# Local attention's operands loaded from channel rows in quarters of 32 partitions, and a high part written in place

## The chip, the cores and the metric

The kernel runs on one core of a Trainium2 chip. The core has a matrix engine (TensorE, PE in the profile; its loads of stationary operands are PEld), three engines for vectors (VectorE, DVE; ScalarE, ACT; GpSimd, POOL) and SyncE (SP), which here issues nearly all DMA transfers. Each engine carries out its own instructions in order; semaphores hold them together. Sixteen DMA engines move the data. The metric is the time of one execution on the device, in microseconds (us); the median of three runs is the kernel's time.

## What is computed

Two attentions with separate inputs and weights, set side by side in the output. Both have 32 heads of 18 channels over 2048 positions; all is float32.

```python
def _A_ref(x, wqkv, wo):                 # x [1, 2048, 576]
    H = 32; Dh = D // H
    W, dil = 8, 2
    qkv = (x @ wqkv).reshape(B, S, 3, H, Dh).transpose(2, 0, 3, 1, 4)
    q, k, v = qkv[0], qkv[1], qkv[2]
    idx = pos[:, None] - off[None, :]    # off = 0, 2, 4 .. 14
    logits = jnp.einsum("bhsd,bhswd->bhsw", q, kg) * scale
    logits = jnp.where(mask[None, None, :, :], logits, -1e9)
    attn = _softmax(logits, axis=-1)
    o = jnp.einsum("bhsw,bhswd->bhsd", attn, vg)
    return o.transpose(0, 2, 1, 3).reshape(B, S, D) @ wo

def _B_ref(x, wqkv, wo):
    ...
    scores = jnp.einsum("bhqd,bhkd->bhqk", q, k) * scale
    p = _softmax(scores, axis=-1)
    o = jnp.einsum("bhqk,bhkd->bhqd", p, v)
    return o.transpose(0, 2, 1, 3).reshape(B, S, D) @ wo

return jnp.concatenate([a, b], axis=-1)
```

A is a local attention: each position looks at itself and at seven earlier positions, two apart (14 positions back at most; kg and vg are keys and values gathered so). B is a full attention.

## The kernel before

**Precision.** Matrix products run in a reduced float32 format. Operands are split into a high part (rounded by a copy) and a low part (the rest), and products are summed as high by high, high by low and low by high.

**Projections (to about 422 us).** x comes in transposed, 576 channels by 2048 positions, in five pieces of rows per 512 positions: four of 128 channels and a last one of 64. For each such group of positions the function `inputs` (L393) loads the pieces and splits them: `split` (L371) rounds on ACT (L372) and subtracts on VectorE or POOL (L373). The last 64 channels are loaded twice, into both halves of the partitions; one half of the tile `xhl` keeps the high part (L407), the other half the low part: ACT writes the high part into a tile `ohi` (L408), and the difference goes to `xhl` (L409). `ohi` has four buffers, which this step shares with the results of the projections: `leave` (L459) copies B's queries and keys out of PSUM (L464), rounds them into `ohi` (L465), takes the low part on POOL (L466) and stores both (L471); `leave_a` (L652) copies a part of A's projection into `ohi` (L654) and stores it to `da` in DRAM (L655). A buffer is free again when its store has landed. The tile `more` holds the raw rows of the last 512 positions of A. `da` has one row per channel: 576 of queries, 576 of keys, 576 of values, each 14 zeros and then 2048 positions.

**Scores (from about 424 us).** B runs in 512 steps: 8 groups of four heads, 4 blocks of 512 queries each, 16 tiles of 128 keys. In a step PE makes four score tiles (L232), which ACT turns into exponentials (L238), and weighs values with those of an earlier step (L704, into `po`). With them PE makes three or four tiles of scores for a later block (L162), of which VectorE takes the maxima (L169); the maxima are turned, split on POOL (L107, L108) and placed beside the queries by eight small loads (L195). Every 16 steps a block ends: ACT copies `po` to `o` (L713), SP loads the four rows of denominators into `den` (L736), due one step later; eight steps after the block's end VectorE takes their reciprocals (L737), SP stores them (L738) and loads them back spread over the partitions as `rec` (L739, due at 13), and POOL multiplies (L740, 18), splits (L741, L742), and SP stores (L732, 26). Twelve loads bring each later group's queries and keys (`stack_loads`, L146 and L147), and one its values (L247).

**A beside B.** A has eight blocks of 256 positions, 54 steps apart, from step 10 + 54 j. Partitions are 32 heads times 4 quarters of 64 positions: partition 32 s + h holds quarter s of head h. For each block the function `local` (L818) plans pieces by step:

- `arrange` (L823): three DMA copies, DRAM to DRAM, from `da` into `dparts`, one each for queries, keys and values. A copy has 576 channels times 4 quarters, each a run of 64 positions (queries) or 78 (keys and values, with the 14 positions before). They are due 24 steps ahead of the block or, where that falls into the first 14 steps of a group, later.
- `fetch` (L829): one load of 128 long rows per tensor (L833), into `aq` (one buffer) and `akv` (two buffers, keys and values by turns); queries at step 0 of the block, keys at 1, values at 28.
- `match`, from step 5: products of queries and keys on POOL (L844) and their sums (L848), last the logits `lg` (L851). VectorE takes maxima over the window (`am`, L862, from step 31), POOL subtracts (L868), ACT takes exponentials, VectorE sums and inverts (L878), POOL scales (L881).
- `weighted`, from step 39: products with the values (L887) and sums (L888 to L890) on POOL; then the split and the stores to `dao` (L902), from which `get` (L912, L914) loads `at` and `ahl` for the product with A's output weights (L1014).

**What sets the order.** Nearly the whole program is written out by hand: `plan` and `later` put functions under step numbers, and `due` calls them in that step. All loads above stand in SP's one queue in that order. A DMA waits on SP for what it needs and, as eight semaphores are used by turns, for the DMA eight places ahead of it; everything behind it waits too.

Of the kernel before, what the change touches and what calls it, by code (L numbers as in the profile page):

```python
# [7 lines left out]
F32 = mybir.dt.float32  # L8
F32R = mybir.dt.float32r
BF16 = mybir.dt.bfloat16  # L10
AF = mybir.ActivationFunctionType
# [5 lines left out]
S = 2048  # L17
D = 576
H = 32
DH = 18  # L20
# [9 lines left out]
NJ = S // AB  # L30
SUB = AB // 4
HALO = DIL * (W - 1)

STEPS = NB * NT
# [9 lines left out]
GAP = 54  # L44

A_FROM = 10
# [5 lines left out]
def ap(t, *dims):  # L52

    return bass.AP(tensor=t.tensor, offset=t.offset, ap=[list(t.ap[0])] + [list(d) for d in dims])


def rows(t, *dims):

    return bass.AP(tensor=t.tensor, offset=t.offset, ap=[list(d) for d in dims])
# [3 lines left out]
def two_attentions(ctx: ExitStack, tc, xa, wa, woa, xb, wb, wob, out):  # L63
# [5 lines left out]
    nc = tc.nc  # L69
    load = nc.sync.dma_start  # L70

    const = ctx.enter_context(tc.tile_pool(name="const", bufs=1))
    dram = ctx.enter_context(tc.tile_pool(name="dram", bufs=1, space=DRAM))
# [9 lines left out]
    def bank(kind=None):  # L83
# [6 lines left out]
    dqk = dram.tile([2, 2 * D, S], F32, name="dqk")  # L90
    dv = dram.tile([NG, 128, NT, 4 * 19], F32, name="dv")


    da = dram.tile([3 * D, HALO + S], F32, name="da")
    dparts = [[dram.tile([4, D, (HALO if n else 0) + SUB], F32, name=f"dpart{n}{j}") for n in range(3)]
              for j in range(NJ)]
    dao = dram.tile([NJ, 2, 4, D, SUB], F32, name="dao")
    drec = dram.tile([NG, NB, 4, 512], F32, name="drec")
    do = dram.tile([2, NG - 1, 128, S], F32, name="do")
# [242 lines left out]
    with (tc.tile_pool(name="x", bufs=1, side="right") as xp,  # L342
# [14 lines left out]
        def staged(src, cols, dims, into, spare=False):  # L357

            n = sum(m for _, m in cols)
            wide = src.shape[1]  # L360
            raws = {}

            def get(c, issue=load):
                t = raws[c] = raw(spare)
                for at, r0, m in [(0, 128 * c, 128)] if c < 4 else [(0, 512, 64), (64, 512, 64)]:
                    issue(ap(t[at : at + m], (n // len(cols), len(cols)), (1, n // len(cols))),
                          rows(src[r0, cols[0][0]], (wide, m), *dims))

            return get, lambda c: into(c, raws[c][:, :n])

        def split(engine, hi, lo, t):  # L371
            nc.scalar.activation(hi, t, AF.Copy)  # L372
            engine.tensor_sub(lo, t, hi)  # L373
# [19 lines left out]
        def inputs(src, b, engine, spare=False):  # L393
            x = [[], [], None]

            def into(c, t):
                if c < 4:
                    hi, lo = (xp.tile([128, 512], F32R, name=nm, bufs=4 * NB) for nm in ("xhi", "xlo"))
                    x[0].append(hi)
                    x[1].append(lo)  # L400
                    split(engine, hi, lo, t)
                else:

                    hl = x[2] = xp.tile([128, 512], F32R, name="xhl", bufs=NB)
                    high = xp.tile([128, 512], F32R, name="ohi", bufs=4)
                    one, other = (slice(64 * (b % 2), 64 * (b % 2) + 64), slice(64 - 64 * (b % 2), 128 - 64 * (b % 2)))
                    nc.scalar.activation(hl[one], t[one], AF.Copy)  # L407
                    nc.scalar.activation(high[other], t[other], AF.Copy)  # L408
                    engine.tensor_sub(hl[other], t[other], high[other])  # L409

            return x, *staged(src, [(512 * b, 512)], [(512, 1), (1, 512)], into, spare)

# [30 lines left out]
        qkv, odd = ExitStack(), ExitStack()  # L443
# [3 lines left out]
        if True:  # L447
# [34 lines left out]
            for c in range(5):  # L482
                one, other = (load, nc.scalar.dma_start) if c % 2 == 0 else (nc.scalar.dma_start, load)
# [159 lines left out]
            for k in range(2, 14):  # L643
                n = 46 if k == 2 else 36 + 4 * k
# [7 lines left out]
            def leave_a(c, b, n, ps):  # L652
                o = xp.tile([128, 512], F32, name="ohi", bufs=4)
                nc.scalar.activation(o[:n], ps, AF.Copy)  # L654
                load(da[128 * c : 128 * c + n, HALO + 512 * b : HALO + 512 * b + 512], o[:n])  # L655
# [23 lines left out]
            for c, b in order:  # L679
                n = min(128, 3 * D - 128 * c)  # L680
                work_list.append(((b % 2, ws[c][0], xas[b][0], slice(0, n), every),
                                  lambda ps, n=n: ps[:n], lambda ps, c=c, b=b, n=n: leave_a(c, b, n, ps)))
# [16 lines left out]
    work = ctx.enter_context(tc.tile_pool(name="work", bufs=1, reuse_waits="tile"))  # L699
# [118 lines left out]
    def local(j):  # L818

        st = {}  # L820
        p0 = AB * j

        def arrange(n):  # L823
            wide = (HALO if n else 0) + SUB
            load(rows(dparts[j][n][0, 0], (wide, D), (D * wide, 4), (1, wide)),
                 rows(da[D * n, HALO + p0 + SUB - wide :], (HALO + S, D), (SUB, 4), (1, wide)))


        def fetch(nm):  # L829
            halo = 0 if nm == "q" else HALO  # L830
            n = DH * (halo + SUB)
            t = st[nm] = work.tile([128, DH, halo + SUB], F32, name="akv" if halo else "aq", bufs=2 if halo else 1)
            load(ap(t, (1, n)), rows(dparts[j]["qkv".index(nm)][0, 0], (n, 128), (1, n)))  # L833

        def window(t, c):

# [46 lines left out]
        def weighted(c):  # L883
            if c == 0:
                st["o"] = work.tile([128, DH, SUB], F32, name="ao", bufs=1)
            at = wide()
            nc.gpsimd.tensor_mul(at, ap(st["lg"], (0, 2), (SUB, W), (1, SUB)), window(st["v"], c))  # L887
            nc.gpsimd.tensor_add(at[:, :, :4], at[:, :, :4], at[:, :, 4:])  # L888
            nc.gpsimd.tensor_add(at[:, :, :2], at[:, :, :2], at[:, :, 2:4])  # L889
            nc.gpsimd.tensor_add(st["o"][:, 2 * c : 2 * c + 2], at[:, :, 0], at[:, :, 1])  # L890
# [10 lines left out]
        def put(i):  # L901
            load(rows(dao[j, i, 0, 0], (DH * SUB, 128), (1, DH * SUB)),  # L902
                 ap(st["parts"][i].bitcast(F32), (1, DH * SUB)))
# [18 lines left out]
        def sums_of_a(h):  # L922
# [3 lines left out]
            if h == 0:  # L926
# [3 lines left out]
            nc.scalar.activation(y, two, AF.Copy)  # L930
            behind_scores.append(lambda: nc.vector.tensor_add(y, one, y))

        pieces = [(0, lambda: fetch("q")), (1, lambda: fetch("k")), (28, lambda: fetch("v")), (33, lower),
                  (35, exponents), (39, share), (60, upper), (61, rest), (64, lambda: put(0)), (66, lambda: put(1))]

        pieces[:0] = [(at, lambda f=f, n=n: f(n)) for f, ats in ((most, (31, 32, 33)), (total, (36, 37, 38)),
                                                                (inverses, (38, 39))) for n, at in enumerate(ats)]
        for c in range(DH // 2):
            pieces.append((5 + 5 * c // 2, lambda c=c: match(c)))
            pieces.append((39 + 5 * c // 2, lambda c=c: weighted(c)))  # L940
        at = A_FROM + GAP * j - 24

        at = max(at, STEPS * (at // STEPS) + 14) - A_FROM - GAP * j
        for n in range(3):
            pieces.append((at + n if j else n - 7, lambda n=n: arrange(n)))
        made = [p - A_FROM - GAP * j for p in MADE[j]]
        for n, ends in enumerate((made[:2], made[2:])):
            pieces.append((max(ends[0] - 8, made[1] + 1 if n else 0), lambda n=n: get(n)))
# [145 lines left out]
    for j in range(NJ):  # L1094
        plan(A_FROM + GAP * j, local(j))
# [15 lines left out]
    rest = NG * NB * PIECES * 2 - early  # L1111
# [24 lines left out]
    while step < ALL:  # L1136
        n, kt = divmod(step, NT)
# [51 lines left out]
```

## Time and profile before

| what | value |
|---|---|
| runs | 1648.64, 1649.69, 1653.81 us |
| median | 1649.69 us |
| profiled execution: its time | 1651.53 us |
| profiled execution: span, first to last instruction | 1649.8 us |
| mean granted TensorE clock | 0.995 |
| bytes read from and written to HBM | 113.16 and 88.12 MB |
| DMA packets, of these under 512 B | 188353, 118384 |

Rows of the profile are read so. A group or a timeline row has the line of the code, the engine, the operation, what is written from what, and how often ("x"). In a timeline the first number is the start in us from the span's start and the second the length; brackets at the end tell how long the engine stood idle before and what released it. SPq rows are DMA issues: their length is the time that SP needed for the issue, not that of the transfer. Rows of tiles give the shortest, median and longest duration in ns and the first and last start. Rows of stretches give the start and end, the length, then the busy time of PE, PEld, DVE, ACT and POOL, each with its number of instructions, then the granted clock (1.00 is full), the DMA engines' busy share and GB/s. "bank" is a PSUM bank with a score or product tile.

### The profile page before, as it was taken

The numbers are of one execution on the slowest core, as the hardware profiler recorded it, in microseconds if no ns is written. First come the engines' busy times: TensorE is split into PE (matmuls) and PEld (weight loads), VectorE is DVE, ScalarE is ACT, GpSimd is POOL, SyncE is SP. The second block draws the span as 40 slices with busy tenths as digits, with TensorE's granted clock in tenths as the row PEclk, the third lists the DMA queues.
The fourth block names the chain that finished last, engine by engine and source line by source line (L and its number), as shares of the span: only waits on it lengthen the run. The fifth ranks groups of instructions, "written<-read, shape, count | busy, mean of one in ns | idle before, by whom it ended". The sixth has DMA issues, their size and how long they took to land.

```text
span 1649.8 us, 33746 instructions
## 1 busy us (share of the span) xinstructions
PE 1632.9 (99%) x12906; PEld 951.6 (58%) x12906; DVE 1392.9 (84%) x2366; ACT 1224.0 (74%) x2419; POOL 960.1 (58%) x792
## 2 busy tenths in 40 slices
PE   9999999999999999999999899999999999999998
PEld 7999879999433444444444344444444444445676
DVE  5199989999899888889888789899899989888533
ACT  7314432111899999999999799999999999998554
POOL 2306642210195996995994993995995997930000
PEclk9999999999999999999999899999999999999999
DMA  9937954522515347167228325826626141033201
GB/s 257 232 113 208 251 164 134 137 89 90 95 47 101 97 120 128 54 150 124 74 66 158 96 82 119 150 74 97 151 87 109 65 133 51 21 121 117 106 37 59
DMA packets 188353, 188.22 MB, mean 114 GB/s; under 512 B 118384, under 2 KB 132208, under 8 KB 186464
## 3 DMA queue, kind: packets, MB, share of 16 engines
q1 hardware_dynamic: 183328, 174.53, 41.6%
q0 software_dynamic: 4032, 10.63, 3.3%
q8 instruction: 101, 1.65, 0.5%
q10 hardware_dynamic: 832, 0.92, 0.2%
q14 instruction: 60, 0.49, 0.1%
HBM read 113.16 MB, written 88.12 MB: 122 GB/s over the span
## 4 chain that ended last, share of the span: by engine, by line
PE 90%; POOL 6%; DMA 1%; DVE 1%; issue 1%; ACT 0%; SPq 0%; POOLq 0%; ACTq 0%; DVEq 0%
PE po L704 27%; PE bank L232 22%; PE bank L325 16%; PE bank L162 13%; PE bank L1014 7%; PE bank L262 5%; POOL pr L844 1%; POOL pr L887 1%; POOL pr L848 1%; DMA den<-o 1%; DVE mx L169 1%; POOL pr L888 1%; POOL pr L889 0%; DMA dqk<-ohi 0%; PE bank L478 0%
## 5 line engine op out<-in xcount | busy, mean ns | idle before, releaser
L169 DVE TENSOR_REDUCE mx<-bank 128x1 f32<-128x512 f32 x2048 | 1287.8, 684 | 146.0 <-PE bank L162 115.4
L238 ACT ACTIVATE e<-bank 128x512 f32<-128x512 f32 x2048 | 1062.1, 606 | 97.0 <-PE bank L232 57.3
L162 PE MATMUL bank<-ks,qs 54*128 54x512 f32 x2048 | 753.5, 423 | 7.1 <-DVE mx L169 6.9
L232 PEld LDWEIGHTS bank<-qs,ks 56*128 56x128 f32 x2048 | 328.4, 186 | 447.4 <-ACT e L238 417.7
L232 PE MATMUL bank<-qs,ks 56*128 56x512 f32 x2048 | 573.0, 426 | 0.0
L704 PE MATMUL po<-e,v 128*19 128x512 f32 x4096 | 538.4, 600 | 0.0
L162 PEld LDWEIGHTS bank<-ks,qs 54*128 54x128 f32 x2048 | 341.3, 185 | 18.0 <-DVE mx L169 11.4
L704 PEld LDWEIGHTS po<-e,v 128*19 128x19 f32 x4096 | 70.6, 97 | 185.7 <-issue 182.9
L844 POOL TENSOR_TENSOR pr<-aq,akv 128x1024 f32<-128x1024 f32 x72 | 158.5, 2202 | 28.1 <-PE bank L232 25.5
L887 POOL TENSOR_TENSOR pr<-lg,akv 128x1024 f32<-128x1024 f32 x72 | 158.3, 2198 | 0.6
L848 POOL TENSOR_TENSOR pr<-pr 128x1024 f32<-128x1024 f32 x64 | 152.5, 2383 | 5.0
L654 ACT ACTIVATE ohi<-bank 128x512 f32<-128x512 f32 (+1 forms) x56 | 30.5, 595 | 147.2 <-issue 115.9
L325 PE MATMUL bank<-xhi,ahi 64*128 64x512 f32 (+1 forms) x448 | 114.3, 390 | 3.1 <-ACT ohi L654 3.1
L325 PE MATMUL bank<-xhi,alo 64*128 64x512 f32 (+1 forms) x448 | 113.3, 390 | 0.0
L325 PE MATMUL bank<-xlo,ahi 64*128 64x512 f32 (+1 forms) x448 | 111.2, 390 | 0.2 <-POOL xlo L373 0.2
L888 POOL TENSOR_TENSOR pr<-pr 128x512 f32<-128x512 f32 x72 | 92.4, 1283 | 5.6
L373 POOL TENSOR_TENSOR alo<-raw,ahi 128x512 fp32r<-128x512 f32 (+1 forms) x14 | 17.6, 1255 | 121.5 <-ACT ahi L372 88.9
L466 POOL TENSOR_TENSOR olo<-olo,ohi 128x512 fp32r<-128x512 f32 x36 | 46.2, 1295 | 64.2 <-ACT ohi L465 50.9
L740 POOL TENSOR_TENSOR o<-o,rec 128x512 f32<-128x512 f32 x29 | 37.4, 1289 | 59.3 <-ACT e L238 23.7
L325 PEld LDWEIGHTS bank<-xhi,ahi 64*128 64x128 f32 (+1 forms) x448 | 65.8, 183 | 5.8 <-ACT ohi L654 3.6
L325 PEld LDWEIGHTS bank<-xhi,alo 64*128 64x128 f32 (+1 forms) x448 | 64.4, 183 | 2.0
L325 PEld LDWEIGHTS bank<-xlo,ahi 64*128 64x128 f32 (+1 forms) x448 | 62.5, 183 | 3.2 <-POOL xlo L373 1.0
(197 smaller groups left out, 1784.5 us busy)
## 6 DMA issues: line engine op xcount, KB each, us to landing
do<-n SPq DMA_DIRECT2D x28, 512.0 KB
da<-ohi SPq DMA_DIRECT2D x52, 256.0 KB
dpart<-da SPq DMA_DIRECT2D x16, 702.0 KB
akv<-dpart SPq DMA_DIRECT2D x16, 702.0 KB
out<-y SPq DMA_DIRECT2D x32, 288.0 KB
qs<-dqk SPq DMA_DIRECT2D x30, 288.0 KB
ks<-dqk SPq DMA_DIRECT2D x30, 288.0 KB
at<-dao SPq DMA_DIRECT2D x64, 128.0 KB
```

The costliest lines, as they stand in the source:

```text
L162: nc.tensor.matmul(ps, qs[at, b, p, 128 * t : 128 * t + 128], ks[at, p, 512 * k : 512 * k + 512], start=True, stop=True)
L169: nc.vector.tensor_reduce(mx[:, r, p, t, k : k + 1], ps, axis=AX.X, op=ALU.max)
L232: nc.tensor.matmul(ps, ks[at, p, 128 * kt : 128 * kt + 128], qs[at, b, p], start=True, stop=True)
L238: nc.scalar.activation(e, ps, AF.Exp, scale=SCALE)
L262: nc.tensor.matmul(ps, a, b, start=c == i == 0, stop=c == 4 and i == 1)
L325: nc.tensor.matmul(ps, a, b, start=start, stop=stop)
L704: nc.tensor.matmul(po[32 * i : 32 * i + 19], vs[g][:, kt, 19 * i : 19 * i + 19], es[i], start=kt == 0, stop=kt == NT - 1)
L844: nc.gpsimd.tensor_mul(pr, ap(st["q"][:, 2 * c], (SUB, 2), (0, W), (1, SUB)), window(st["k"], c))
L848: nc.gpsimd.tensor_add(st["pr"], st["pr"], pr)
L887: nc.gpsimd.tensor_mul(at, ap(st["lg"], (0, 2), (SUB, W), (1, SUB)), window(st["v"], c))
L888: nc.gpsimd.tensor_add(at[:, :, :4], at[:, :, :4], at[:, :, 4:])
L1014: nc.tensor.matmul(ps, a, b, start=start, stop=stop)
```

## The change

Two edits.

The copies of `arrange` and the tensors `dparts` are gone. `fetch` loads straight from `da` into the same tiles: for each tensor four loads, one per quarter, each of 32 heads (partitions) times 18 channels times 64 or 78 positions. For blocks 1 to 7 the quarters of the queries are due 18, 16, 14 and 12 steps ahead of the block's start and those of the keys 10, 8, 6 and 4 ahead; for block 0, 9 to 6 and 5 to 2 ahead. Those of the values are due at steps 16, 18, 20 and 22 of the block.

In `inputs` the tile from `ohi` is gone. ACT writes the high part of the second half into `xhl` itself, and the difference overwrites it there. This holds for the last rows of A and of B, eight times in all.

```diff
     da = dram.tile([3 * D, HALO + S], F32, name="da")
-    dparts = [[dram.tile([4, D, (HALO if n else 0) + SUB], F32, name=f"dpart{n}{j}") for n in range(3)]
-              for j in range(NJ)]
...
                     hl = x[2] = xp.tile([128, 512], F32R, name="xhl", bufs=NB)
-                    high = xp.tile([128, 512], F32R, name="ohi", bufs=4)
                     one, other = (slice(64 * (b % 2), 64 * (b % 2) + 64), slice(64 - 64 * (b % 2), 128 - 64 * (b % 2)))
                     nc.scalar.activation(hl[one], t[one], AF.Copy)
-                    nc.scalar.activation(high[other], t[other], AF.Copy)
-                    engine.tensor_sub(hl[other], t[other], high[other])
+                    nc.scalar.activation(hl[other], t[other], AF.Copy)
+                    engine.tensor_sub(hl[other], t[other], hl[other])
...
-        def arrange(n):
-            wide = (HALO if n else 0) + SUB
-            load(rows(dparts[j][n][0, 0], (wide, D), (D * wide, 4), (1, wide)),
-                 rows(da[D * n, HALO + p0 + SUB - wide :], (HALO + S, D), (SUB, 4), (1, wide)))
-
-
-        def fetch(nm):
+
+        def fetch(nm, s):
             halo = 0 if nm == "q" else HALO
-            n = DH * (halo + SUB)
-            t = st[nm] = work.tile([128, DH, halo + SUB], F32, name="akv" if halo else "aq", bufs=2 if halo else 1)
-            load(ap(t, (1, n)), rows(dparts[j]["qkv".index(nm)][0, 0], (n, 128), (1, n)))
+            if s == 0:
+                st[nm] = work.tile([128, DH, halo + SUB], F32, name="akv" if halo else "aq", bufs=2 if halo else 1)
+            load(st[nm][32 * s : 32 * s + 32],
+                 rows(da[D * "qkv".index(nm), HALO + p0 + SUB * s - halo :],
+                      (DH * (HALO + S), H), (HALO + S, DH), (1, halo + SUB)))
...
-        pieces = [(0, lambda: fetch("q")), (1, lambda: fetch("k")), (28, lambda: fetch("v")), (33, lower),
-                  (35, exponents), (39, share), (60, upper), (61, rest), (64, lambda: put(0)), (66, lambda: put(1))]
+        pieces = [(33, lower), (35, exponents), (39, share), (60, upper), (61, rest), (64, lambda: put(0)), (66, lambda: put(1))]
...
-        at = A_FROM + GAP * j - 24
-
-        at = max(at, STEPS * (at // STEPS) + 14) - A_FROM - GAP * j
-        for n in range(3):
-            pieces.append((at + n if j else n - 7, lambda n=n: arrange(n)))
+
+        for nm, at, apart in (("q", -18, 2), ("k", -10, 2)) if j else (("q", -9, 1), ("k", -5, 1)):
+            pieces += [(at + apart * i, lambda nm=nm, i=i: fetch(nm, i)) for i in range(4)]
+        pieces += [(16 + 2 * i, lambda i=i: fetch("v", i)) for i in range(4)]
```

## The prediction

> **What bounds the kernel now.** The page's first rows give the engine: TensorE (PE) is busy for all but 16.9 us of the span.
>
> ```profile
> span 1649.8 us, 33746 instructions
> PE 1632.9 (99%) x12906; PEld 951.6 (58%) x12906; DVE 1392.9 (84%) x2366; ACT 1224.0 (74%) x2419; POOL 960.1 (58%) x792
> ```
>
> The change takes no matmul away, and the changed program has every instruction of PE, DVE, ACT and POOL in the same order with the same shapes; only SyncE's DMA queue (SP) is reordered and an operand renamed. So it can gain only where PE waits. The waits of PE's matmuls, whole kernel:
>
> ```profile
> PE bank L162 <- DVE mx L169: 6.9, 4, 6.3
> PE bank L325 <- ACT ohi L654: 3.1, 1, 3.1
> PE bank L478 <- DVE raw L476: 1.5, 1, 1.5
> ```
>
> Columns are us in total, times, longest. Two single waits matter, 6.3 and 3.1 us. I cut the score stage (from 424 us) into stretches to place the first:
>
> ```profile
> 424.00:906.00 482.00, 481.83 (x3530) 205.05 (x3530) 435.32 (x742) 455.50 (x890) 363.50 (x273) 1.00 0.49 103
> 906.00:925.00 19.00, 12.74 (x71) 4.78 (x68) 8.64 (x15) 9.31 (x19) 18.06 (x16) 0.73 0.65 135
> 925.00:1545.00 620.00, 620.00 (x4727) 278.99 (x4721) 561.01 (x958) 570.28 (x1115) 446.06 (x343) 1.00 0.39 100
> ```
>
> First PE's busy time and matmuls, at the end clock, DMA share, GB/s. In 1100 us PE has one hole, at 906 to 925, and there the clock is 0.73. The chain of waits and the timelines of DVE, PE and SP say what made it:
>
> ```profile
> 888.41 10.25 SPq L825 DMA_DIRECT2D dpart<-da  x3
> 898.76 7.56 SPq L736 DMA_DIRECT2D den<-o  x1
> ...
> 913.23 0.25 DVE L737 RECIPROCAL den<-den 128x16 f32<-128x16 f32 x1 [7.66 <-DMA den<-o]
> ...
> 914.08 1.38 PE L162 MATMUL bank<-ks,qs 54*128 54x512 f32 x2 [6.26 <-DVE mx L169]
> ```
>
> SP issued the three arranging copies of A's block 4, was busy with them for 10.25 us, and then needed 7.56 us to issue the 8 KB of denominators behind them. These landed at 913.2. DVE, in order, had the reciprocal of them ahead of its maxima, so the maxima waited 7.66 us, no bank came free, and PE stood 6.26 us. The median issue of that small DMA is 589 ns:
>
> ```profile
> L736 SPq DMA_DIRECT2D den<-o x29: 569/589/7560, 457.8 to 1480.5; - x29
> ```
>
> The copies are what stood ahead of it. What the DMA engines moved from 888.4 to 898.8 and to 913.2:
>
> ```profile
> DMA packets 3435, 1.82 MB, mean 175 GB/s; under 512 B 3177, under 2 KB 3177, under 8 KB 3364
> DMA packets 4055, 1.22 MB, mean 85 GB/s; under 512 B 4053, under 2 KB 4053, under 8 KB 4053
> ```
>
> Of 7490 packets 7230 are under 512 B. The three copies have 576 x 4 runs each, 6912 in all, of 256 or 312 B.
>
> **What the hole costs.** It is more than 6.26 us, because PE comes back at half clock:
>
> ```profile
> 914.00:916.00 2.00, 1.92 (x6) 1.32 (x6) 2.00 (x5) 0.66 (x2) 1.84 (x4) 0.50 0.47 151
> 922.00:924.00 2.00, 2.00 (x19) 0.74 (x16) 1.78 (x4) 1.96 (x5) 1.84 (x3) 1.00 0.64 244
> ```
>
> From 906 to 925 PE did 71 matmuls; at 7.32 to 7.62 per us (3530 in 482, 4727 in 620) they need 9.3 to 9.7 us of those 19. Lost: 9.3 to 9.7. The chain gives it more closely, by the weighings that come once in a step:
>
> ```profile
> 895.86 0.98 PE po L704 x8
> ...
> 924.57 0.98 PE po L704 x8
> ...
> 926.69 0.98 PE po L704 x8
> ```
>
> A step is 2.12 us; the nine steps from 895.86 to 924.57 should take 19.0 and took 28.7. I use 9.7.
>
> **The change, part by part.** (1) Three arranging copies per block of 256 positions go. Each block loses 6912 DRAM-to-DRAM runs and three loads of long rows, and gets twelve loads of 32 x 18 = 576 runs of the same 256 or 312 B, 6912 again, now straight into SBUF. SP's price:
>
> ```profile
> L825 SPq DMA_DIRECT2D dpart<-da x24: 530/2232/8103, 423.6 to 1251.4; - x24
> L833 SPq DMA_DIRECT2D akv<-dpart x16: 347/424/836, 444.3 to 1355.1; - x16
> L833 SPq DMA_DIRECT2D aq<-dpart x8: 345/469/522, 443.9 to 1298.3; - x8
> L912 SPq DMA_DIRECT2D at<-dao x64: 366/508/2697, 588.8 to 1495.3; - x64
> ```
>
> Nearest to a quarter is the load of at (512 runs of 256 B, 508 ns); 576/2304 of a copy is 558 ns. Twelve quarters: 6.1 to 6.7 us of SP per block, against 3 x 2.23 + 2 x 0.42 + 0.47 = 8.0. SP gains about 1.5 us per block, off PE's path.
>
> For the DMA engines the trace has no 32-partition load of such rows. Bounds: from 1098 to 1104, where four at and two ahl loads ran, 2583 short packets passed in 6 us, 2.3 ns each; the copies' 6912 took at most 913.2 - 888.4 = 24.8 us, 3.6 ns each.
>
> ```profile
> DMA packets 2641, 0.72 MB, mean 120 GB/s; under 512 B 2583, under 2 KB 2583, under 8 KB 2641
> ```
>
> So 1.3 to 2.1 us for a quarter; I take 2, by the copies, which read the same rows. Quarters are due two steps (4.2 us) apart, so they leave the queue half free.
>
> (2) What stands ahead of each denominator load in the changed order of SP: at the place that stalls, one quarter of queries; elsewhere the reciprocal of the previous group (rec), at most two quarters, in one group also a stack load. Two quarters are 4 us, where the copies were 24.8. The reciprocal comes seven steps, 14.8 us, after the load is due, so 10 us stay. The hole goes: -9.7. Lower bound of this gain 0 (it was not the copies), no more than 9.7.
>
> (3) New waits: the quarters of queries and keys overwrite buffers that POOL reads until its last product of the block before, and SP stands in order. POOL's products of blocks 1, 2 and 3:
>
> ```profile
> L844 POOL TENSOR_TENSOR pr<-aq,akv x9: 2196/2199/2202, 580.6 to 623.0; 128x1024 f32<-128x1024 f32 x9
> L844 POOL TENSOR_TENSOR pr<-aq,akv x9: 2189/2204/2217, 697.6 to 740.4; 128x1024 f32<-128x1024 f32 x9
> L844 POOL TENSOR_TENSOR pr<-aq,akv x9: 2192/2196/2218, 819.4 to 865.0; 128x1024 f32<-128x1024 f32 x9
> ```
>
> ```profile
> 637.61 5.84 SPq L736 DMA_DIRECT2D den<-o  x1
> ```
>
> Block 1's end at 625.2. Block 2's first quarter stands right behind this denominator load, which SP reached behind copies; without them the sums of step 97 let it go at about 635: 10 us to spare, the least of all blocks; block 4's (867.2 against 888) has 21. The last keys are due nine steps, 19 us, before POOL's first product; values come 12 to 6 steps earlier than before and 17 steps, 36 us, before their use. For block 0 there are no copies to wait for any more, so POOL may start some us before its 449.6; DVE's maxima hold its second half where it is. Cost 0; if POOL were 10 us late, the placements of maxima behind the quarter would be late with it.
>
> (4) The in-place high part. L408 took one of four "ohi" buffers and waited for a store to give it back; ACT's next leaves waited again, then PE:
>
> ```profile
> 217.44 0.63 ACT L408 ACTIVATE ohi<-raw 64x512 fp32r<-64x512 f32 x1 [6.59 <-DMA dqk<-ohi]
> ...
> 222.11 0.60 ACT L654 ACTIVATE ohi<-bank 128x512 f32<-128x512 f32 x1 [2.82 <-DMA dqk<-ohi]
> ...
> 227.03 1.28 POOL L409 TENSOR_TENSOR xhl<-more,ohi 64x512 fp32r<-64x512 f32 x1
> ```
>
> ```profile
> 205.00:210.00 5.00, 5.00 (x47) 4.07 (x44) 4.96 (x11) 4.31 (x8) 4.43 (x4) 1.00 0.34 109
> 215.00:220.00 5.00, 4.64 (x42) 3.43 (x38) 4.70 (x8) 1.82 (x3) 1.72 (x2) 1.00 0.90 266
> 220.00:225.00 5.00, 2.07 (x13) 1.41 (x15) 1.65 (x3) 2.89 (x6) 2.54 (x3) 0.92 0.78 259
> 225.00:230.00 5.00, 5.00 (x34) 3.94 (x34) 3.23 (x5) 1.50 (x3) 3.31 (x3) 0.74 0.58 170
> ```
>
> From 215 to 230 PE did 89 matmuls where 141 fit at the pace of 205 to 210: 5.5 us lost. Without L408's buffer the first leave takes the store of 217.4 and the second the next, and PE's bank is free by about 219.3; PE wants it at 222.7 - 3.1 = 219.6. But the third leave now needs the store that landed at 222.1, and behind it on ACT stand the last piece of x and its halves: leave to 222.7, another 223.3, then 0.63 x 3, then POOL's 1.28 for the last rows, 226.5 with the handovers. Before, that ended at 228.3. So I take 1.8 less 0.3 for handovers not seen, 1.5 us. It lies between 5.5 and 0: every later user of the ring takes a buffer that came free earlier than its old one, so no loss. The six other rows made in place show no wait of their size before, and cost 0.
>
> Here a rule bears on the size. The Trainium skill, "TensorE: Matmul & The Clock Gate", part 1, says the clock halves after an idle window of about 3.4 us; the trace halves it after 6.26 and partly after 3.12 us. By the rule the pieces that are left, each near 1 us, would not halve it, and the gain stays 1.5; were it halved as in 225 to 230 (34 matmuls for 47), that would take 1.4 back and the gain be near 0.
>
> **Sum.** The profiled execution took 1651.53 us, 1.7 beyond its span. 1651.5 - 9.7 - 1.5 = 1640.3. It lies 1.8 above the median of the runs shown; against the median the sum is 1638.5. I say 1639.
>
> **Rivals.** (B) The hole stays, since something else filled the queue: 1649.7 - 1.5 = 1648. The packets speak against it (6912 of 7490). Chance 0.08.
>
> (C) The wait moves to POOL. At steps 316 to 330 (about 1147 to 1180) eight quarters, 16 us at 2 us each, fall among twelve stack loads. There the queue is full already (4.06 us for one issue). The logits that POOL makes next end at 1249.5, and DVE reads them at 1254.5:
>
> ```profile
> 1160.13 4.06 SPq L914 DMA_DIRECT2D ahl<-dao  x1
> ```
>
> ```profile
> 1248.23 1.29 POOL L851 TENSOR_TENSOR lg<-pr 128x512 f32<-128x512 f32 x1
> ...
> 1254.45 0.42 DVE L862 TENSOR_TENSOR am<-lg 128x256 f32<-128x256 f32 x1
> ```
>
> If the reciprocals (rec) come 10 us later, POOL, in order, ends so much later, DVE waits for it ahead of its maxima, and PE for DVE. The 5 us between these rows cover half, 5 are left, with the clock about 6: 1645. Chance 0.13.
>
> (D) Slower: quarters fill the queue more than the copies did. One place: every denominator load with quarters ahead of it. It decides from about 5 to 7 us per quarter (two or three ahead use up the 14.8 us). Two holes of 9.7 give 1640 + 19 = 1659, one in each of seven blocks 1707. For it speaks that only 32 partitions are written at a time; against it the at loads, 64 columns per run at 2.3 ns a packet. Chance 0.09.
> The Trainium skill, "DMA: Bandwidth & Descriptors", section "Rules for kernel authors", says that transfers to separate parts of the partitions gain nothing over one transfer of 128; no run here shows it yet.
>
> **How the numbers follow.** Forecast 0.70, B 0.08, C 0.13, D 0.09. A measurement of this kernel can tell 0.3%, 4.9 us: faster is below 1644.7. The forecast lies there nearly whole, and half of C: 0.75. Same: B, half of C, a little of the forecast: 0.16. Slower: D, 0.09. The forecast's own range goes from 1634 (edit 4 gives all of 5.5) to 1643; for 8 in 10 it has to take in C and just touch B: 1633 to 1648.
>
> **What would show it.** Right: PE's hole at 906 gone and clock 1.00 there; no reciprocal waiting for its load; PE's wait for L654 gone with 1 us pieces for POOL left near 222; a quarter's issue near 0.5 us. Wrong: a new PE wait with DVE behind POOL near 1250 (C), den loads of several us behind quarters (D), a hole of the same size at 906 (B).

## The result and the profile after

The changed kernel takes 1637.69 us, median of five runs (1637.48 to 1638.67). The kernel before, run beside it again, takes 1653.04 (five runs, 1648.64 to 1653.81). The ratio is 0.9917, with the interval 0.9902 to 0.9932: 0.8% faster, 14 us (the ratio is one of means; the two medians lie 15 us apart). The profiled execution took 1637.69 us, its span is 1635.9 where it was 1649.8.

The page's first rows:

```profile
span 1635.9 us, 33786 instructions
...
PE 1627.4 (99%) x12906; PEld 944.2 (58%) x12906; DVE 1393.1 (85%) x2366; ACT 1223.1 (75%) x2419; POOL 959.4 (59%) x792
```

PE stands 8.5 us of the span, where it stood 16.9. The other 5.5 of the 13.9 us are in its busy time, 1632.9 before and 1627.4 now, with the same matmuls: time at half clock counts as busy.

The same stretches as before (columns: PE's busy time and matmuls first, at the end clock, DMA share, GB/s):

```profile
424.00:906.00 482.00, 482.00 (x3539) 205.38 (x3537) 436.55 (x745) 457.14 (x894) 369.77 (x276) 1.00 0.36 88
906.00:925.00 19.00, 19.00 (x150) 8.90 (x149) 16.98 (x29) 17.26 (x36) 18.06 (x17) 1.00 0.12 27
925.00:1545.00 620.00, 620.00 (x4775) 282.29 (x4776) 552.44 (x946) 563.28 (x1101) 439.47 (x340) 1.00 0.32 88
```

From 906 to 925 PE now does 150 matmuls instead of 71, at clock 1.00. What PE's matmuls still wait for (us in total, times, longest):

```profile
PE bank L474 <- DVE raw L472: 1.5, 1, 1.5
PE bank L322 <- ACT olo L460: 1.1, 1, 1.1
PE bank L159 <- DVE mx L166: 0.5, 2, 0.2
```

The wait for `ohi` (3.1 us before) is gone, and of the 6.9 us of waits for the maxima 0.5 are left. The 1.1 us for `olo` were not there before. The queue of SP at the place of the old hole (start, length of the issue):

```profile
880.60 0.63 SPq L824 DMA_DIRECT2D aq<-da  x1
882.95 0.57 SPq L732 DMA_DIRECT2D den<-o  x1
883.58 4.48 SPq L824 DMA_DIRECT2D aq<-da  x2
```

One quarter stands ahead of the denominators, and their load is issued in 0.57 us instead of 7.56. In VectorE's timeline the reciprocal then has no bracket, it waits for nothing:

```profile
900.92 0.24 DVE L733 RECIPROCAL den<-den 128x16 f32<-128x16 f32 x1
```

The same holds at all 29 places: the longest issue of that load is 632 ns (shortest, median, longest in ns; first and last start):

```profile
L732 SPq DMA_DIRECT2D den<-o x29: 565/594/632, 454.6 to 1466.4; - x29
```

Where the 13.9 us came from is read from the starts of the weighings, one per step, numbered alike in both traces. The score stage starts 3.3 us earlier (420.83 where it was 424.12), the lead grows by 0.9 us between steps 97 and 106, by 9.7 us at steps 218 to 220, and ends at 13.9. So there are three sources: the projections, a small one near 650 us, and the hole.

### The profile page after: what moved, and what is told of

Same layout as the page of the kernel before. It is cut to its first block, busy times and chain, and to the rows that moved or that the text cites. A ratio compares the mean times of both kernels' runs of the same rounds, so it can differ in the third digit from the quotient of the medians.

```text
span 1635.9 us, 33786 instructions
## 1 busy us (share of the span) xinstructions
PE 1627.4 (99%) x12906; PEld 944.2 (58%) x12906; DVE 1393.1 (85%) x2366; ACT 1223.1 (75%) x2419; POOL 959.4 (59%) x792
## 4 chain that ended last, share of the span: by engine, by line
PE 96%; DMA 1%; POOL 1%; DVE 1%; issue 0%; ACT 0%; SPq 0%; POOLq 0%; ACTq 0%; DVEq 0%
PE po L700 31%; PE bank L229 25%; PE bank L322 14%; PE bank L159 14%; PE bank L1005 7%; PE bank L259 5%; DMA dqk<-olo 1%; POOL xlo L370 1%; PE bank L474 0%; DMA more<-xa 0%; DVE mx L166 0%; POOL olo L462 0%; DMA out<-y 0%; PE bank L980 0%; ACT vs L540 0%
## 5 line engine op out<-in xcount | busy, mean ns | idle before, releaser
L1005 PE MATMUL bank<-wohi,at 64*128 64x288 f32 x512 | 63.8, 295 | 0.0
```

The costliest lines, as they stand in the source:

```text
L1005: nc.tensor.matmul(ps, a, b, start=start, stop=stop)
```

## The experiments

All times below are set against the kernel before, run on the same chip in the same session; its median was 1651.95 us beside the first four kernels below, 1652.82 beside the others and 1647.73 beside the one with halves. Single executions of one kernel differ by several us (1647.86 to 1656.78 for the kernel before in the first session), so only the intervals and the places in the traces are used.

### Each edit alone

The in-place high part alone:

```diff
-                    high = xp.tile([128, 512], F32R, name="ohi", bufs=4)
...
+                    nc.scalar.activation(hl[other], t[other], AF.Copy)
+                    engine.tensor_sub(hl[other], t[other], hl[other])
```

> The kernel before with the in-place high part alone. Theory: the hole at 906 stays as it is (PE's wait for mx 6.3 us, den issue about 7.5 us), and the whole 3.3 us by which the score stage starts earlier in the changed kernel come from this edit: score stage from about 420.9 instead of 424.1, time 3 to 4 us below before, ratio 0.9978. By the prediction's own term of 1.5 us: start at 422.6, ratio 0.9991. Rival: the earlier start comes from SP, which has other loads in its queue, or is chance: start at 424, ratio 1.000.

Measured: 1648.3 us, ratio 0.9984 (0.9974 to 0.9995), so 0.8 to 4.3 us. By the time alone the expected 3.3 us and the prediction's 1.5 are both possible; the start of the score stage decides between them. The hole stays, with a longest wait of 5.6 us where it was 6.3; from PE's waits and the first weighing of the score stage:

```profile
PE bank L162 <- DVE mx L169: 6.1, 3, 5.6
```

```profile
420.93 1.05 PE L703 MATMUL po<-e,v 128*19 128x512 f32 x8
```

The score stage starts at 420.93, so the earlier start comes with this edit alone.

The quarters alone (the other half of the diff, with `ohi` as before):

> The kernel before with the quarters alone. Theory: the hole at 906 is gone (9.7 us) and with it the small loss at steps 97 to 106 (1.1 us): 10.8 us below before, ratio 0.9935; the stall of the projections near 220 stays, and the score stage starts at about 424. Rival: the quarters bring part of the earlier start too, then the time is 12 to 14 us below before, ratio 0.992, and the wait for L654 is below 2 us. Rival: the hole went for another reason than the loads; then PE keeps a wait of 3 us or more for mx.

Measured: 1641.55 us, ratio 0.994 (0.9924 to 0.9955), so 7.4 to 12.6 us, around the 10.8 expected. The stretch of the hole and the start of the score stage:

```profile
906.00:925.00 19.00, 19.00 (x150) 8.91 (x149) 17.13 (x29) 17.77 (x37) 18.11 (x16) 1.00 0.38 106
```

```profile
424.45 1.05 PE L701 MATMUL po<-e,v 128*19 128x512 f32 x8
```

Step by step the lead over the kernel before is -0.1 at step 97, 0.8 at 106 and 10.0 at 220. Hole and small loss belong to the quarters, the start does not. ACT still waits for its `ohi` buffer, as long as before (6.59 there):

```profile
218.42 0.63 ACT L405 ACTIVATE ohi<-raw 64x512 fp32r<-64x512 f32 x1 [6.76 <-DMA dqk<-ohi]
```

The two medians give 3.7 and 10.4 us, 14.1 together, and the two ratios 2.6 and 9.9, 12.5 together: within the intervals, the edits add up.

### Only the place in the queue

The kernel before, with the copies of block 4 due six steps later and everything else left:

```diff
         at = max(at, STEPS * (at // STEPS) + 14) - A_FROM - GAP * j
+        if j == 4:
+            at += 6
```

> The kernel before with the three arranging copies of block 4 due six steps later, so that they stand behind the load of the denominators and not ahead of it; every load and every byte stays. Theory (the hole is a matter of order in the queue): that load is issued in about 0.6 us, lands some 20 us earlier, PE's wait of 6.3 us goes and the time falls by 9 to 10 us, ratio 0.994. Rival (the copies' 6912 short packets disturb whatever runs beside them): the next small transfers, the store and load of the reciprocals, are late in its place, POOL waits about 10 us for rec near 930, and PE loses 5 us or more again: ratio 0.997 to 1.000.

Measured: 1644.19 us, ratio 0.9947 (0.9931 to 0.9963), 6.1 to 11.4 us. In SP's queue the load now stands ahead of the copies:

```profile
891.62 0.58 SPq L736 DMA_DIRECT2D den<-o  x1
892.26 8.68 SPq L825 DMA_DIRECT2D dpart<-da  x2
```

The step starts show the clean number: the lead goes from -2.7 at step 215 to 7.0 at step 220, 9.7 us, as with the quarters. The -2.7 were there before that place; 1.7 of them come from the projections, where this execution waited longer for a buffer of `olo`. PE's waits:

```profile
PE bank L325 <- ACT olo L464: 4.1, 2, 3.6
...
PE bank L162 <- DVE mx L169: 1.0, 3, 0.5
```

So the hole was a matter of order in one queue. The 6912 short runs did PE no harm here once nothing urgent stood behind them. The rival's late reciprocals did not come: no wait took the hole's place on PE.

### The price of a quarter

The changed kernel, with block 4's quarters of queries and keys due together, ahead of the denominators:

```diff
...
+        for nm, at, apart in (("q", -18, 2), ("k", -10, 2)) if j not in (0, 4) else (("q", -20, 0), ("k", -19, 0)) if j else (("q", -9, 1), ("k", -5, 1)):
```

> The changed kernel with block 4's eight quarters of queries and keys due together in two steps, so that seven of them stand ahead of the denominators. It measures the price of a quarter. At 2 us each 14 us stand ahead, the load lands about 15 us after it was due and DVE waits 0 to 1 us: time within 1 us of the changed kernel. At 1.3 us each no wait at all. At 3.6 us, or if 32 partitions take much longer than 128, 25 us stand ahead, DVE waits about 8 us, PE has a hole of 6 to 7 us and the time is 9 to 10 us above the changed kernel.

Measured: 1638.2 us, ratio 0.9927 (0.9911 to 0.9942), the changed kernel's time. SP's queue:

```profile
885.24 9.16 SPq L824 DMA_DIRECT2D aq<-da  x4
894.44 3.27 SPq L824 DMA_DIRECT2D akv<-da  x4
897.81 0.59 SPq L732 DMA_DIRECT2D den<-o  x1
```

All eight quarters stand ahead, one more than the expectation counted. They were issued from 885.24 to 897.71, 1.6 us each. VectorE's reciprocal follows without a wait:

```profile
905.06 0.24 DVE L733 RECIPROCAL den<-den 128x16 f32<-128x16 f32 x1
```

The load was issued 7 us ahead of that. With eight quarters ahead there is still room, so rival D of the prediction (a quarter at 5 to 7 us) is out. Two of this kernel's six executions took 1642 to 1643 us; the profiled one is of these, and has a 2.4 us wait for `olo` in the projections: of the 4.5 us by which its span is longer than the changed kernel's, 2.8 are there when the score stage starts, before any of these quarters.

The four quarters of every tensor in one step, in the changed kernel:

```diff
-        for nm, at, apart in (("q", -18, 2), ("k", -10, 2)) if j else (("q", -9, 1), ("k", -5, 1)):
+        for nm, at, apart in (("q", -18, 0), ("k", -10, 0)) if j else (("q", -9, 1), ("k", -5, 1)):
...
-        pieces += [(16 + 2 * i, lambda i=i: fetch("v", i)) for i in range(4)]
+        pieces += [(16, lambda i=i: fetch("v", i)) for i in range(4)]
```

> The changed kernel with the four quarters of each tensor due in one step and not two steps apart. By the 1.8 us per quarter that the burst of seven showed, four take 7.3 us, still less than the 14.8 us: theory: same time as the changed kernel within 1 us, no wait of DVE for the denominators. Rival (the spreading is what removed the hole): a wait for the denominators of several us and a time 5 to 10 us higher.

(The 1.8 us in it took the burst for seven quarters; by eight it is 1.6, and four take 6.2 us.) Measured: 1638.26 us, ratio 0.9914 (0.9901 to 0.9927). The changed kernel beside it:

> The changed kernel once more, unaltered, as the measure for the three kernels run beside it. Its time should be 1637.5 to 1638.7 us as before; some executions may take 4 to 5 us more, as two of the six of the kernel with the burst did, where PE waits 2 to 4 us for the low parts (olo) near 190 to 198.

It took 1638.35 us, ratio 0.9914 with the same interval. Spreading the quarters two steps apart is worth nothing here; the longest issue of the denominators with them together is 1.5 us:

```profile
L732 SPq DMA_DIRECT2D den<-o x29: 564/593/1484, 454.8 to 1466.8; - x29
```

### Quarters, halves or one load

If spreading does not matter, does the cut into quarters? One load of 128 partitions per tensor, same runs and bytes:

```diff
             if s == 0:
...
+                load(st[nm], rows(da[D * "qkv".index(nm), HALO + p0 - halo :],
+                                  (SUB, 4), (DH * (HALO + S), H), (HALO + S, DH), (1, halo + SUB)))
```

> The changed kernel with one load of all 128 partitions per tensor (2304 runs) at the place of its first quarter, in place of the four quarters. Theory: what costs is the number of runs ahead of a waiting load, 2304 at most here, 5 to 8 us by the copies' 2.3 to 3.6 ns, less than the 14.8 us there are: no hole, time within 2 us of the changed kernel, and one issue costs SP about 2.2 us as a copy did. Rival (the quarters matter): a load whose outermost count is four is carried by few of the sixteen DMA engines, takes 20 us or more, the denominators behind it land late, PE has a hole of 5 us or more near 906 and the time is 7 to 10 us above the changed kernel.

Measured: 1664.77 us, ratio 1.008 (1.0062 to 1.0098), 26 us above the changed kernel, and 13 above the kernel before. SP's queue at one place, and VectorE's wait there:

```profile
596.18 0.55 SPq L824 DMA_DIRECT2D akv<-da  x1
596.84 12.53 SPq L732 DMA_DIRECT2D den<-o  x1
```

```profile
612.95 0.25 DVE L733 RECIPROCAL den<-den 128x16 f32<-128x16 f32 x1 [5.95 <-DMA den<-o]
```

It is the picture of the old hole, with one load ahead instead of three copies. While nothing but that load runs, the stretch and the DMA view show:

```profile
598.00:608.00 10.00, 10.00 (x80) 4.67 (x76) 8.38 (x15) 9.74 (x20) 9.70 (x7) 1.00 0.31 54
```

```profile
DMA packets 1720, 0.54 MB, mean 54 GB/s; under 512 B 1720, under 2 KB 1720, under 8 KB 1720
```

A DMA share of 0.31 and 172 packets per us: at that pace 2304 runs take 13.4 us. While SP's queue is blocked, the sixteen DMA engines together are busy for less than a third of the time. PE waits for the maxima in five places, and in four for `at`, an operand of A's last product:

```profile
PE bank L159 <- DVE mx L166: 15.1, 5, 5.6
PE bank L1004 <- DMA at<-dao: 7.2, 4, 4.7
```

The direction is as the rival had it, but its 7 to 10 us were too few, and its place was wrong. It counted one hole near 906, and there is none: from 906 to 925 PE is busy throughout, with 139 matmuls at clock 1.00. The four longest waits lie near 614, 747, 1069 and 1271 us. The theory's 2.2 us per issue was wrong too: SP issues the load in 0.55 us, and the load behind it pays.

To tell the shape from the size, two loads of 64 partitions:

```diff
...
+            if s % 2 == 0:
+                load(st[nm][32 * s : 32 * s + 64],
+                     rows(da[D * "qkv".index(nm), HALO + p0 + SUB * s - halo :],
+                          (SUB, 2), (DH * (HALO + S), H), (HALO + S, DH), (1, halo + SUB)))
```

> The changed kernel with two loads of 64 partitions (1152 runs each) per tensor, each at the place of its first quarter: the outermost count of the source is 2, where it was 4 for the whole load and 32 for a quarter. Theory (the outermost count sets how many of the 16 DMA engines carry a load): a lone half shows a DMA share near 2/16, 0.12 to 0.16, and at the whole load's pace per engine (172 runs per us on four) takes 13 us or more; two of them close together leave no less time ahead of the small loads than a whole one, so the time is 20 us or more above the changed kernel, at least as slow as with whole loads. Rival (what counts is the number of runs in one load, or the 128 partitions): half the runs, half the delay: 0 to 13 us above the changed kernel, DMA share near 0.3 or higher.

Measured: 1776.33 us, ratio 1.0764 (1.0716 to 1.0811). Half the runs per load made it far slower still, by 7.6% against the kernel before. While one half runs nearly alone:

```profile
638.00:648.00 10.00, 8.98 (x54) 4.68 (x58) 6.60 (x12) 4.48 (x9) 2.93 (x2) 0.66 0.16 28
```

```profile
DMA packets 860, 0.28 MB, mean 28 GB/s; under 512 B 859, under 2 KB 859, under 8 KB 859
```

86 packets per us at share 0.16, where the whole load had 172 at 0.31: exactly half. Per count of the outermost dimension both make 43 runs per us (172/4 and 86/2). So the pace goes with the outermost count of the source, 4 or 2. It would go as well with the number of partitions, 128 or 64, but the quarters speak against that: with 32 partitions they would then run at 43 per us and take 13 us each, and the burst showed 1.6. The quarters' outermost count is 32. No load of 128 partitions with a larger outermost count was run, so that the count alone frees a load is argued and not shown. VectorE now waits for the denominators at eleven places:

```profile
DVE den L733 <- DMA den<-o: 78.8, 11, 15.3
```

The Trainium skill, "DMA: Bandwidth & Descriptors", section "Why a DMA increments its semaphore by 16 and not by 1", says the number of DMA engines is the largest up to 16 that divides the slowest dimension of both sides; by that rule, as an estimate, 4 and 2 of 16 carry these loads, shares of 0.25 and 0.13. The runs agree in the ratio and lie 0.03 to 0.06 above in the share; how many engines carried a load is not in the trace. The other rule of the Trainium skill, which the prediction weighed (one transfer of 128 partitions instead of parts), did not hold for the whole load as it stands here, with an outermost count of 4: it cost 26 us.

### More buffers

Five instead of four buffers for `ohi` and `olo`:

```diff
...
-                hi = xp.tile([128, 512], F32R, name="ohi", bufs=4)
-                lo = low.tile([128, 512], F32R, name="olo", bufs=4)
+                hi = xp.tile([128, 512], F32R, name="ohi", bufs=5)
+                lo = low.tile([128, 512], F32R, name="olo", bufs=5)
...
```

> The changed kernel with five instead of four buffers each for ohi and olo. Theory: what is left to lose in the projections, and what differs from one execution to the next, is the wait for a buffer of these rings, 1.1 us in the changed kernel's profile and 2.4 to 3.6 in others; with five buffers PE's wait for olo near 190 to 198 falls below 0.3 us: 1 to 3 us faster than the changed kernel, 1635 to 1637, with a smaller spread. Rival: the stores themselves are the limit (the DMA engines are 0.8 to 0.9 busy there), the wait only moves some stores later: same time within 0.5 us.

Measured: 1638.15 us, ratio 0.9914 (0.9901 to 0.9927), the time of the changed kernel. The rival was right; the wait is still there:

```profile
PE bank L322 <- ACT olo L460: 1.2, 1, 1.2
```

No version run here beats the changed kernel.

## Why the prediction was right, step by step

**The hole** (forecast -9.7). Right in cause and size: 9.7 us by the step starts, with the quarters and also when only the copies' place changed. The lower bound of 0 (not the copies) is excluded by the latter. (Nine steps of 2.12 us are 19.1 and not 19.0, so the prediction's chain itself gives 9.6.)

**A second wait for the same load** was in rows that the prediction had quoted for another purpose, and its gain was left out. Block 2's copies stood ahead of a denominator load too (SP, then VectorE, before):

```profile
628.37 9.14 SPq L825 DMA_DIRECT2D dpart<-da  x3
637.61 5.84 SPq L736 DMA_DIRECT2D den<-o  x1
```

```profile
651.73 0.25 DVE L737 RECIPROCAL den<-den 128x16 f32<-128x16 f32 x1 [1.08 <-DMA den<-o]
```

The maxima were 1.1 us late there; the changed kernel and the quarters alone both gain 0.9 us at this place. A third long issue of this load before, 7.2 us at 1044.9, had no wait of VectorE behind it and cost nothing.

**The in-place high part** (forecast -1.5, between 0 and 5.5). A buffer of the ring given back is the mechanism, as forecast, but the wait that counted was another one and the size was too small: 3.3 us between the two profiled executions, 2.6 by the repeated runs of this edit alone. The three profiled kernels that keep `high` start the score stage at 424.12, 424.45 and 425.78, the eight that don't between 419.44 and 423.63, 421.1 in the mean: 3.7 us. The step that failed is "the six other rows made in place show no wait of their size before, and cost 0". They did not wait themselves, but they held a buffer that another instruction waited for, 34 us ahead of the place that was costed. ACT, before and after:

```profile
183.09 0.63 ACT L465 ACTIVATE ohi<-olo 128x512 fp32r<-128x512 f32 x1 [5.73 <-DMA dqk<-ohi]
```

```profile
177.30 0.63 ACT L461 ACTIVATE ohi<-olo 128x512 fp32r<-128x512 f32 x1
...
211.28 0.63 ACT L404 ACTIVATE xhl<-raw 64x512 fp32r<-64x512 f32 x1
...
217.56 1.08 ACT L650 ACTIVATE ohi<-bank 128x512 f32<-128x512 f32 x2 [4.99 <-DMA dqk<-olo]
...
221.26 1.08 ACT L650 ACTIVATE ohi<-bank 128x512 f32<-128x512 f32 x2 [1.58 <-POOL xlo L370]
```

L465 at 171.98 and 173.13, L408 at 174.31 and L465 at 176.15 had taken the four buffers of the ring; without L408 the next L465 finds one free. Behind its wait POOL was late with the last rows of the next piece and with the low parts, 191.3 instead of 187.7:

```profile
191.31 1.31 POOL L409 TENSOR_TENSOR xhl<-raw,ohi 64x512 fp32r<-64x512 f32 x1
```

```profile
187.69 1.30 POOL L405 TENSOR_TENSOR xhl<-raw,xhl 64x512 fp32r<-64x512 f32 x1
...
224.25 1.28 POOL L405 TENSOR_TENSOR xhl<-more,xhl 64x512 fp32r<-64x512 f32 x1
```

and SP, whose stores wait for the low parts, came 4 us later to all that follows. Before, then after:

```profile
201.76 2.38 SPq L195 DMA_DIRECT2D qs<-mh  x4
...
211.67 1.18 SPq L471 DMA_DIRECT2D dqk<-ohi  x2
```

```profile
197.79 2.31 SPq L192 DMA_DIRECT2D qs<-mh  x4
...
207.31 1.75 SPq L467 DMA_DIRECT2D dqk<-ohi  x2
```

So the forecast's next limit, that "the third leave now needs the store that landed at 222.1", did not hold: that store was issued 4 us earlier. At 211.28 L404 follows without the 6.59 us that L408 waited, the first two leaves go together, and the third and fourth (221.26) wait for POOL and no store. The last rows end at 225.5 instead of 226.5. No half clock follows (before, 34 matmuls at 0.74 from 225 to 230):

```profile
220.00:225.00 5.00, 4.90 (x43) 3.71 (x41) 4.95 (x8) 2.86 (x5) 3.81 (x4) 1.00 0.51 158
225.00:230.00 5.00, 5.00 (x48) 4.30 (x46) 4.29 (x7) 0.00 (x0) 0.53 (x1) 1.00 0.17 45
```

PE loses 0.1 us there, where pieces of about 1 us were expected. Counted along PE's matmuls, numbered alike in both traces, the place from 218 to 228 alone gave 4.9 us: the changed kernel comes to it 1.6 us behind the kernel before and leaves it 3.3 ahead. The 1.6 were lost earlier, most of them in the wait for `olo` of 1.1 us at 194.5. The second profile of the changed kernel, which lacks that wait, comes there 0.2 behind and leaves 4.7 ahead. So the worth of the edit differs with the execution: with only the copies moved, and `high` kept, PE came there 6.5 us late and lost 4.9 us less than the kernel before. SP begins the loads of the last group (`more`) at 208.5 to 209.2 us in the three profiled kernels that keep `high`, and at 204.1 to 206.2 in the eight that don't, so the earlier loads go with this edit and not with one execution. That they follow from the buffer taken at 174.31 is read from the rows above; no run gave back that one buffer alone.

**The price of a quarter.** SP's issue was a little dearer than the 558 ns estimated:

```profile
L824 SPq DMA_DIRECT2D akv<-da x64: 550/600/2035, 423.1 to 1338.2; - x64
```

Twelve take 7.2 us per block where the copies and loads took 8.0: 0.8 us saved and not 1.5, off PE's path. For the DMA engines the burst showed 1.6 us; the prediction had bounds of 1.3 and 2.1 and took 2. Its argument was weaker than its number: it compared runs of the same length, and did not see that the shape of the load decides. With 64 partitions per load, what rival D describes would have come true.

**New waits** (forecast 0). None reached PE. POOL starts on block 0 at 434.3 instead of 449.6, as it needs no copies any more:

```profile
434.31 4.35 POOL L837 TENSOR_TENSOR pr<-aq,akv 128x1024 f32<-128x1024 f32 x2 [13.46 <-DMA akv<-da]
```

POOL's waits for `rec` are 14.4 us in two places, 11.4 in one before, and PE has no wait behind them: rival C did not occur. The time to spare ahead of block 2's first quarter was shorter than the 10 us forecast: the denominators went out at 627.36, not near 635, and block 1's products ended at 621.7, which leaves 6 us. Rival B (the hole stays) is excluded by the stretch at 906.

**The sum.** 1651.5 - 9.7 - 1.5 made 1640.3 against the profiled execution; with 0.9 for the second wait and 3.3 in place of 1.5 it is 1637.6, and the profiled execution took 1637.7. The step down to 1639 for the median was without ground: further runs of the kernel before have their medians at 1651.95, 1652.82 and 1647.73, and the profiled execution stands within these. It happened to offset part of what was missing.

## What to carry to other kernels

A small load that something urgent waits for pays for what stands ahead of it in its queue. Look at the longest issue of such a load beside its median, see whether an engine then waits for it, and ask first whether it can simply go ahead; here a move by six steps gave the same 9.7 us as a rewrite of the loads. When a load is cut up or merged, count the outermost dimension of both sides before the bytes: against four loads with 32 outermost, the same 2304 runs cost 26 us more as one load with 4, and more than 100 us as two loads with 2. When an edit gives back a buffer of a ring, look for every waiter on that ring, and not only for the instruction that is taken out: here the wait that counted was another one's, 34 us earlier.

## What was not expected of the hardware

- The pace of a load of short runs was 43 runs per us and unit of the outermost count, for counts of 4 and 2 alike, with the DMA engines only 0.31 and 0.16 busy. The quarters, with a count of 32, took 1.6 us for 576 runs.
- The issue of such a load took SP no longer than that of a quarter (medians 0.55 and 0.60 us). What grew was the issue of the 8 KB load behind it, to 12.5 us, so the row that looks expensive is not the one that causes it.
- PE's wait for `olo` in the projections differs between executions of the same code (1.1 us and none in two profiles of the changed kernel, 2.4 in the burst kernel, whose projections are the same). The score stages of these three executions start at 420.83, 419.44 and 423.63 us.
